# Retention and a rational FFN on one core: later chunks go through TensorE in pairs, with zero products in its waits and a new table of ranks

## The chip, the cores and the metric

The kernel runs on one core of one Trainium2 chip. The metric is the time of one execution on the device, in microseconds (us). Engines are named as in the profile: PE is TensorE (PEld its weight loads), DVE is VectorE, ACT is ScalarE, POOL is GpSimd, SP is SyncE, whose queue issues every DMA of this kernel.

## The reference

Retention (linear attention with a decay per head) over 4 batches, 8 heads, 768 tokens and 64 dimensions; its output, as 3072 tokens of 512 values, goes through a feed-forward layer of 2048 with a rational activation.

```python
gamma = 1.0 - 2.0 ** (-5.0 - np.arange(H))
for t in range(S):
    state = gamma[None, :, None, None] * state + np.einsum('bhd,bhe->bhde', k[:, :, t], v[:, :, t])
    y[:, :, t] = scale * np.einsum('bhd,bhde->bhe', q[:, :, t], state)
...
h = x @ w_in
P = a[0] + a[1] * h + a[2] * h**2 + a[3] * h**3
Q = 1.0 + np.abs(b[0]) * np.abs(h) + np.abs(b[1]) * h**2
out = (P / (Q + 1e-06)) @ w_out
```

## The kernel before

**Chunks.** The 768 tokens are cut into 6 chunks of 128, and chunk i = 4n + b is the n-th of batch b. The four first chunks (n = 0) have no state and go in a form of their own. Each of the 20 later chunks makes two bursts of small 64x64 products on PE, four of which run side by side in quarters of the array. The first burst (L350, L358) holds the scores of both halves of the chunk (16 products into pa) and the outer products of k and v (16, or 8 in the last chunk, into the other half of the same two banks). Then DVE masks the scores (aT), adds the outer products to the state (mid, after), all in steps of 256 columns. The second burst (L376, 32 products into px) recalls from state and mid and multiplies aT with v. DVE scales px, ACT rounds it into xh, DVE takes the remainder xl; POOL scales k ahead of it (L439) and the state behind it.

**Slots.** Four chunks give 512 columns of x. The FFN is a list of 96 slots k, each one column block n of x and one block f of 128 hidden units. In slot k the hidden block, called h_k here, is twelve products of 512 columns into a bank ph (L665: w high with xh, w high with xl, w low with xh). ACT, POOL and DVE turn ph into g: an Abs (L718), a linear step called the second activation here (L727 on ACT or L723 on POOL), a third (L733), a product on POOL (L738), five steps on DVE and two more on ACT (L747, L750); ACT rounds g into gh (L762), POOL takes the remainder gl (L766). The output block, O_k here, is again twelve products, into four banks po (L680: gh with w high, gh with w low, gl with w high). There are two banks ph, so h_(k+2) waits until slot k is done with its bank. The first 32 slots go through the column blocks 0 and 1 in halves of 8 hidden blocks.

**Weights.** w_in and w_out come as 64-bit numbers, 0.52 MB for each of 32 blocks. Each is decoded: two ACT steps (L625, L629), two DVE steps (L635, L638), a split into the high part on ACT (L644) and the rest on POOL (L647).

**The order.** Nothing runs in the order in which it is written. Each piece of work is a step with engines, a cost, its predecessors, buffers and a rank; `Plan.order` (below) picks at each time the ready step with the lowest rank on the engine that is free first, and emits it. The tables LOADS, RANKS and OFFSETS set the ranks. The engines then run their own instructions strictly in the emitted order. Before the first h the planner puts bf16 products of zeros into PE's waits (L893).

**Banks.** Of the eight PSUM banks, two are for ph, four for po, and two (b2, b3) for everything else: pa, px, pk. Until a given number of h blocks has begun (EARLY), the po banks serve too.

Of the kernel before, what the change touches and what calls it, by code (L numbers as in the profile page):

```python
# [7 lines left out]
F32 = mybir.dt.float32  # L8
# [16 lines left out]
COLD = 2600, 3200  # L25
# [19 lines left out]
class Plan:  # L45
# [10 lines left out]
    def step(  # L56
        self, engines, cost, run, after=(), rank=0.0, takes=(), uses=(), tiled=False, kind=None
    ):
        rank += OFFSETS.get(kind, 0.0)
# [70 lines left out]
    def order(self, emit):  # L130
# [6 lines left out]
        open_ = []  # L137

        def enter(x):
            x.known = 0  # L140
            for a, early in x.after:
                x.known = max(x.known, a.start if early is None else a.end - early + WAKE)
            open_.append(x)
# [5 lines left out]
        while left:  # L149
# [5 lines left out]
            by_engine = {}  # L155
            for x in open_:
                t = self.ready(x)
                if t is None:
                    continue
                for e in x.engines:  # L160
# [15 lines left out]
            open_.remove(x)  # L176
# [8 lines left out]
def tile_retention_rational_ffn(  # L185
# [29 lines left out]
    HF = NF // 2  # L215
# [20 lines left out]
    zeros = ff.tile([P, DM], F32, name="o", bufs=BUFS["o"]).bitcast(BF16)[:, :TB]  # L236
# [27 lines left out]
    def pairs():  # L264
        names = free_banks()
        return [names[i : i + 2] for i in range(0, len(names) - 1, 2)]

# [77 lines left out]
    def scores_outer(st, last):  # L345
        for aj in range(NP):
            for r in range(2):
                for e in range(2):
                    h = 4 * (aj // 2) + 2 * r + aj % 2
                    nc.tensor.matmul(  # L350
                        st["pa"][e][half(r), aj], st["kT"][half(e), h], st["qT"][half(e), h],
                        start=True, stop=True, skip_group_check=True,
                    )
        for aj in range(NP):
            for r in range(2):
                for e in range(1 if last else 2):
                    h = 4 * (aj // 2) + 2 * r + aj % 2
                    nc.tensor.matmul(  # L358
                        st["pk"][e][half(r), aj], st["k"][half(e), h], st["v"][half(e), h],
# [3 lines left out]
    def recall_values(st, own):  # L363
        for what in range(2):
            for e in range(2):
                for a in range(2):
                    for j in range(2):
                        for r in range(2):
                            aj, h = 2 * a + j, 4 * a + 2 * r + j
                            if what:  # L370
                                x = st["v"][half(r), h] if r == e else st["v2"][half(r), aj]
                                y = st["aT"][e][half(r), aj]
                            else:
                                x = (st["mid"] if e else own)[half(r), aj]
                                y = st["qT"][half(r), h] if r == e else st["q2T"][half(r), aj]
                            nc.tensor.matmul(  # L376
                                st["px"][r][half(j), a * P + e * D : a * P + (e + 1) * D], x, y,
                                start=(not what and e == 0 and a == 0), stop=what == 1,
                                skip_group_check=True,
                            )  # L380
# [3 lines left out]
    def x_parts(st, i, r):  # L384
        n, b = divmod(i, B)
        t = slice(b * P, (b + 1) * P)
        xh, xl = (y.rearrange("p (a r) t -> p r a t", r=2)[:, r, :, t] for y in x_tiles[n])
        return st["px"][r][:, : TB // 2].rearrange("p (a t) -> p a t", t=P), xh, xl
# [19 lines left out]
    def attention(i, rank, load_rank, gate):  # L408

        st, (n, b) = {}, divmod(i, B)  # L410
        c, own = n, state[:, b]
        buf, got = {}, {}

        def part(m, src, shape, rank):
            tag = BORROWED.get(i, {}).get(m)
            buf[m] = Buffer(tag or m)

            def dst():
                if tag:
                    full = ff.tile([P, TB], F32, name=m, tag=tag, bufs=BUFS[tag])  # L420
                    st[m] = full.rearrange("p (a b) -> p a b", b=shape[2])
                else:
                    st[m] = at.tile(shape, F32, name=m, bufs=BUFS[m])
                return st[m]

            nbytes = 4 * P * shape[1] * shape[2]
            got[m], _ = load(dst, lambda: src[b, c - 1] if c else src[b], nbytes, rank, [buf[m]])

        kshape = [P, H, D] if c else [P, NP, P]
        part("kT", kT if c else kT0, kshape, load_rank)  # L430
        part("qT", qT if c else qT0, kshape, load_rank + 0.01)
        part("v", v if c else v0, [P, H, D], load_rank + 0.02)
        part("k", kk if c else kk0, [P, H, D], load_rank + 0.015 if c else LATER)
        if c:
            part("q2T", q2T, [P, NP, D], load_rank + 0.03)
            part("v2", v2, [P, NP, D], load_rank + 0.04)

        def scale_k(_):
            nc.gpsimd.tensor_mul(  # L439
                st["k"], st["k"], kdec_sb[:, min(c, 1)].unsqueeze(2).broadcast_to([P, H, D])  # L440
            )

        K = step(
            ("POOL",), (1000, 1043), scale_k, [got["k"], ready["few"]], rank, uses=[buf["k"]], kind="V"
        )

        pa, aT = Buffer("psum", pairs), [Buffer("aT") for _ in range(2)]
        before = bursts.get(i - 2 if i < B else i - 1)
        turn = before and (before, None)

        def run_scores(_):
            banks = [psum(pa, s, "pa") for s in range(2)]
            if c:
                st["pa"], st["pk"] = (
                    [x[:, y].rearrange("p (h t) -> p h t", t=D) for x in banks]
                    for y in (slice(0, TB // 2), slice(TB // 2, TB))
                )
                scores_outer(st, c == C - 1)
            else:
                st["pa"] = [x[:, : 6 * D].rearrange("p (j t) -> p j t", t=3 * D) for x in banks]  # L460
                first_scores(st)

        S = step(
            ("PE",), (900, 800) if c else (830, 700), run_scores,
            [got["kT"], got["qT"], gate, turn] + ([K, got["v"]] if c else []), rank, [pa],
            [buf[m] for m in (("kT", "qT", "k", "v") if c else ("kT", "qT"))], True, "S",
        )
        M = []
        for s in range(2):

            def mask(_, s=s):
                aT_ = at.tile([P, 6 * D], F32, name="aT", bufs=BUFS["aT"])
                if c:
                    by = mask_sb[:, s]
                    aT_ = aT_[:, : 4 * D].rearrange("p (h t) -> p h t", t=D)
                else:
                    by = masks[s].rearrange("p (j t) -> p j t", t=3 * D)
                    aT_ = aT_.rearrange("p (j t) -> p j t", t=3 * D)
                st.setdefault("aT", {})[s] = aT_
                nc.vector.tensor_mul(aT_, st["pa"][s], by)  # L480
# [3 lines left out]
                    ("DVE",), (335, 420) if c else (470, 550), mask,  # L484
                    [S, ready["mask"] if c else mask_loads[s]], rank,
# [557 lines left out]
```

## Time and profile before

| | |
|---|---|
| median of 3 runs | 621.4 us (620.86 to 621.76) |
| the profiled execution | 622.29 us |
| its span, first to last instruction | 620.5 us |
| mean granted TensorE clock | 0.989 |
| PE busy | 601.5 us, 97% |
| DVE, ACT, POOL busy | 72%, 68%, 56% |
| HBM read, written | 50.21 MB, 8.39 MB |
| weights, per block | 512 KB, 7.6 us from issue to landing |

The span is what the views below divide; the 1.8 us between it and the time of the execution lie around it. A busy time counts overlapping instructions once. In a group's row the mean is that of one instruction from start to end; products on PE overlap, so twelve of them take less than twelve means. The chain of waits is followed back from the last instruction, and its rows add up without overlap.

### The profile page before, as it was taken

How to read it: one execution, taken by the hardware profiler on the slowest of the kernel's cores; microseconds unless marked ns; L12 is line 12 of the kernel's file. 1: busy time of each engine (PE TensorE's matmuls, PEld its weight loads, DVE VectorE, ACT ScalarE, POOL GpSimd, SP SyncE). 2: the span in 40 equal slices, each digit the busy share in tenths (PEclk: the TensorE clock that was granted, in tenths of full speed). 3: DMA queues.
4: the chain of work that ended last, by engine and by line, in shares of the span. 5: the costliest groups of instructions: out<-in, count | busy, mean ns of one | idle time of the engine just before them, and what ended most of it. 6: DMA issues, size and time to landing. Idle time of an engine off the chain costs nothing.

```text
span 620.5 us, 13030 instructions
## 1 busy us (share of the span) xinstructions
PE 601.5 (97%) x5155; PEld 485.9 (78%) x5155; DVE 449.1 (72%) x743; ACT 421.6 (68%) x700; POOL 347.0 (56%) x303
## 2 busy tenths in 40 slices
PE   8858999999999999999999999999999999999997
PEld 4736877888887888887888888888888888888885
DVE  3689788999979867767766776667766666666662
ACT  1687779999965555565666766666666666776772
POOL 2387677998867675654544545444444444444442
PEclk9968999999999999999999999999999999999999
DMA  8999631003024330224411222112311100100001
GB/s 304 411 414 414 233 86 69 1 1 135 1 86 155 120 120 17 69 69 121 130 43 52 103 73 66 35 52 69 120 52 36 34 1 0 61 9 1 1 0 69
DMA packets 30733, 59.44 MB, mean 96 GB/s; under 512 B 3536, under 2 KB 8912, under 8 KB 30672
## 3 DMA queue, kind: packets, MB, share of 16 engines
q1 hardware_dynamic: 30672, 58.62, 26.8%
q8 instruction: 40, 0.66, 0.4%
q14 instruction: 21, 0.17, 0.1%
HBM read 50.21 MB, written 8.39 MB: 94 GB/s over the span
## 4 chain that ended last, share of the span: by engine, by line
PE 88%; POOL 2%; DVE 1%; ACT 1%; issue 1%; POOLq 0%; DVEq 0%; ACTq 0%
PE po L680 41%; PE ph L665 41%; PE px L376 3%; PE pa L350 2%; PE pa L358 1%; POOL w L647 1%; POOL gl L766 1%; POOL q L738 0%; ACT ph L750 0%; POOL s L723 0%; ACT s L747 0%; DVE q L754 0%; DVE p L756 0%; DVE ph L755 0%; ACT gh L762 0%
## 5 line engine op out<-in xcount | busy, mean ns | idle before, releaser
L665 PE MATMUL ph<-xh,w 128*128 128x512 f32 (+2 forms) x776 | 209.0, 392 | 3.4 <-DVE p L756 2.3
L680 PE MATMUL po<-w,gh 128*128 128x512 f32 x768 | 203.4, 397 | 6.2 <-ACT gh L762 5.3
L738 POOL TENSOR_TENSOR q<-q,s 128x512 f32<-128x512 f32 x96 | 124.2, 1294 | 147.0 <-ACT s L727 144.3
L680 PEld LDWEIGHTS po<-w,gh 128*128 128x128 f32 x768 | 143.0, 189 | 37.6 <-ACT gh L762 5.4
L665 PEld LDWEIGHTS ph<-xh,w 128*128 128x128 f32 x776 | 144.2, 189 | 35.3 <-DVE p L756 4.1
L766 POOL TENSOR_TENSOR gl<-p,gh 128x512 fp32r<-128x512 f32 x96 | 124.1, 1292 | 27.5 <-ACT gh L762 18.0
L754 DVE SCALAR_TENSOR_TENSOR q<-q,small,ph 128x512 f32<-128x512 f32 x96 | 71.6, 745 | 93.7 <-ACT ph L750 91.8
L718 ACT ACTIVATE q<-ph 128x512 f32<-128x512 f32 x96 | 57.3, 596 | 87.7 <-PE ph L665 87.3
L680 PE MATMUL po<-w,gl 128*128 128x512 f32 x384 | 111.6, 392 | 0.9 <-POOL gl L766 0.9
L665 PE MATMUL ph<-xl,w 128*128 128x512 f32 (+2 forms) x388 | 104.0, 390 | 0.0
L747 ACT ACTIVATE s<-q,small 128x512 f32<-128x512 f32 x96 | 69.5, 724 | 49.2 <-POOL q L738 49.2
L741 DVE TENSOR_TENSOR p<-ph,p 128x512 f32<-128x512 f32 x96 | 65.8, 685 | 30.2 <-ACT p L733 29.1
L680 PEld LDWEIGHTS po<-w,gl 128*128 128x128 f32 x384 | 72.6, 189 | 16.8 <-POOL gl L766 1.7
L665 PEld LDWEIGHTS ph<-xl,w 128*128 128x128 f32 x388 | 73.2, 189 | 15.3
L733 ACT ACTIVATE p<-ph,small 128x512 f32<-128x512 f32 x96 | 74.3, 774 | 2.1 <-POOL gl L766 2.1
L742 DVE SCALAR_TENSOR_TENSOR p<-p,small,ph 128x512 f32<-128x512 f32 x96 | 71.8, 748 | 3.4
L762 ACT CAST gh<-p 128x512 fp32r<-128x512 f32 x96 | 59.2, 617 | 20.1 <-PE po L680 13.0
L755 DVE SCALAR_TENSOR_TENSOR ph<-p,small,ph 128x512 f32<-128x512 f32 x96 | 71.9, 749 | 0.0
L756 DVE SCALAR_TENSOR_TENSOR p<-q,ph 128x512 f32<-128x512 f32 x96 | 65.9, 686 | 3.3
L750 ACT ACTIVATE ph<-s 128x512 f32<-128x512 f32 x96 | 57.8, 602 | 3.7
L647 POOL TENSOR_TENSOR w<-t,w 128x512 fp32r<-128x512 f32 x32 | 41.2, 1293 | 19.8 <-ACT w L644 10.8
L727 ACT ACTIVATE s<-q,small 128x512 f32<-128x512 f32 x61 | 49.7, 814 | 0.3
(53 smaller groups left out, 445.8 us busy)
## 6 DMA issues: line engine op xcount, KB each, us to landing
raw<-in_w_in SPq DMA_DIRECT2D x16, 512.0 KB, 7.6
raw<-in_w_out SPq DMA_DIRECT2D x16, 512.0 KB, 7.8
kT<-in_kT SPq DMA_DIRECT2D x24, 256.0 KB, 3.3
qT<-in_qT SPq DMA_DIRECT2D x24, 256.0 KB, 3.2
v<-in_v SPq DMA_DIRECT2D x24, 256.0 KB, 3.9
k<-in_k SPq DMA_DIRECT2D x24, 256.0 KB, 3.6
out<-o SPq DMA_DIRECT2D x24, 256.0 KB, 2.6
q2T<-in_q2T SPq DMA_DIRECT2D x20, 128.0 KB, 3.2
```

The costliest lines, as they stand in the source:

```text
L665: nc.tensor.matmul(cell["ph"][:, t0:t1], w[0, f][:, part, kt * P : (kt + 1) * P], x[:, kt, t0:t1], start=(i == 0), stop=(i == 3 * NP - 1),)
L680: nc.tensor.matmul(o_tiles[n][tt], g_[:, tt * P : (tt + 1) * P], w[1, f][:, part], start=(first and m == 0), stop=(last and m == 2),)
L733: nc.scalar.activation(cell["p"], cell["ph"], AF.Identity, bias=par_sb[:, 2:3], scale=par_sb[:, 3:4])
L738: nc.gpsimd.tensor_mul(cell["q"], cell["q"], cell["s"])
L741: nc.vector.tensor_mul(cell["p"], cell["ph"], cell["p"])
L742: nc.vector.scalar_tensor_tensor(cell["p"], cell["p"], par_sb[:, 1:2], cell["ph"], ALU.add, ALU.mult)
L747: nc.scalar.activation(cell["s"], cell["q"], AF.Abs_reciprocal_sqrt, bias=qcon[:, 0:1])
L754: nc.vector.scalar_tensor_tensor(q_, q_, qcon[:, 0:1], ph_, ALU.add, ALU.mult)
L755: nc.vector.scalar_tensor_tensor(ph_, p_, par_sb[:, 0:1], ph_, ALU.add, ALU.mult)
L756: nc.vector.scalar_tensor_tensor(p_, q_, 2.0, ph_, ALU.subtract, ALU.mult, reverse0=True)
L762: nc.scalar.copy(cell["gh"], cell["p"])
L766: nc.gpsimd.tensor_sub(cell["gl"], cell["p"], cell["gh"].bitcast(F32))
```

## The change

Chunks 4 to 23 are taken in pairs (two batches of the same n). A pair makes three bursts: the scores of both chunks (32 products, a bank for each half), the outer products of both (32, or 16 at the end, in banks of their own), the recall of both (64). Each DVE, ACT and POOL step behind them covers both chunks, so 512 columns and not 256. There are only two banks for pa, pk and px of one pair behind the start, so each burst enters the banks that the one before has left. Some loads share buffers with tiles that are free by then (`more`, `again`).

```diff
-    def scores_outer(st, last):
+    def scores(st):
+        for x in range(st["n"]):
+            for aj, r, h in heads():
...
+    def outer(st, last):
+        for x in range(st["n"]):
...
+    def later_chunks(i, n, rank, load_rank, gate):
+        more = "o" if c == 1 else "t"
+        small_ops = ((335, 420), (571, 613)) if n == 1 else ((600, 685), (1000, 1043))
...
+        pa = Buffer("psum", pairs)
+        pk = Buffer("psum", pairs) if n == 2 else pa
...
+        if n == 2:
+            O = step(
+                ("PE",), (1000, 900), run_outer, [*K, *ins["v"], (S, None)], rank, [pk],
+                held["k"] + held["v"], True, "S",
+            )
...
+                by = mask_sb[:, e].unsqueeze(1).broadcast_to([P, n, NP, D])
+                nc.vector.tensor_mul(st["aT"][e], st["pa"][e], by)
...
+        R = step(
+            ("PE",), (1000, 900) if n == 1 else (1860, 1760), run_rest,
...
+                many = 2 if built >= PAIRS else 1
+                later_chunks(
+                    built, many, RANKS.get(built, starts[built] + 0.5), LOADS.get(built, starts[built] / 100),
+                    gate,
+                )
```

Products of zeros now go into every wait of PE that the planner expects to be over 0.9 us, also behind the first h: into the bank that comes next, or with start off into an open po bank, to which they add zero.

```diff
-                for _ in range(min(10, int(gap / 430))):
-                    nc.tensor.matmul(idle, zeros[:, :P], zeros, start=True, stop=True)
+            if engine == "PE" and gap > 900:
+                spare[0] = min(12, int(gap / FILL))
+                if not begun(1):
...
+                    fill(idle, True)
+                elif open_po:
+                    fill(open_po[0], False)
```

In the emitted order there are 38 of them: 12 and 10 among the first four chunks, 11 ahead of h_1, 3 ahead of O_0 and 2 ahead of the scores of the second pair. Before there were 23, all ahead of h_0.

The tables are new: LOADS, RANKS, OFFSETS, a nudge for each of some 400 steps, three buffers t in place of two, EARLY 4, and a list of the slots whose second activation is on POOL.

```diff
-        engines = ("ACT", "POOL") if k < SHARED else ("ACT",)
-        A2 = turn("A2", step(engines, {"ACT": (720, 820), "POOL": (771, 771)}, a2, [A1, ready["babs"]], k, [s], [q], kind="A2"))
+        A2 = turn("A2", step(by("A2", k), {"ACT": (720, 820), "POOL": (771, 771)}, a2, [A1, ready["babs"]], k, [s], [q], kind="A2"))
...
+        rank += OFFSETS.get(kind, 0.0) + NUDGES.get(len(self.steps), 0.0)
...
+ENGINES = {
+    ("A2", 0): "POOL", ("A2", 7): "POOL", ("A2", 8): "POOL", ("A2", 9): "POOL",
```

That list has 10 slots (0, 7, 8, 9, 15, 16, 21, 23, 26, 29); before, POOL had 35 second activations, all in the first 40 slots, among them every one of the slots 10 to 21. The first weight of w_in is now the fourth load on SP (it was the twentieth). The last copies out of po begin on DVE and end on ACT (before the other way round). An alternative form of DVE's steps (`aside`) is in the code, but no slot of the list uses it.

What the tables do is seen in the order of instructions. First PE where the chunks with n = 3 begin (pa are scores, pk outer products, px recall). Before, behind h_38, chunk 12:

```order
L350 MATMUL pa<-qT,kT 64x64 x16
L358 MATMUL pa<-v,k 64x64 x16
L680 MATMUL po<-w,gh 128x512 x8
L680 MATMUL po<-w,gl 128x512 x4
L665 MATMUL ph<-xh,w 128x512 x4
L665 MATMUL ph<-xl,w 128x512 x4
L665 MATMUL ph<-xh,w 128x512 x4
L680 MATMUL po<-w,gh 128x512 x8
L680 MATMUL po<-w,gl 128x512 x4
L665 MATMUL ph<-xh,w 128x512 x4
L665 MATMUL ph<-xl,w 128x512 x4
L665 MATMUL ph<-xh,w 128x512 x4
```

Here the recall burst of the one chunk follows. Now, behind h_39, chunks 12 and 13 together:

```order
L369 MATMUL pa<-qT,kT 64x64 x32
L821 MATMUL po<-w,gh 128x512 x8
L821 MATMUL po<-w,gl 128x512 x4
L378 MATMUL pk<-v,k 64x64 x32
L804 MATMUL ph<-xh,w 128x512 x4
L804 MATMUL ph<-xl,w 128x512 x4
L804 MATMUL ph<-xh,w 128x512 x4
L399 MATMUL px<-qT,state 64x64
L399 MATMUL px<-q2T,state 64x64
```

The outer products have a burst of their own, one block behind the scores, and the recall of both chunks stands one block behind that.

Second, ACT from the first Abs to the first gh (q, p, s, gh are slot steps, t, u, w decode steps). Before, without its first two rows:

```order
L733 ACTIVATE p<-ph,small 128x512
L625 ACTIVATE t<-raw,small 128x512
L629 ACTIVATE u<-raw 128x512
L718 ACTIVATE q<-ph 128x512
L644 CAST w<-t 128x512
L747 ACTIVATE s<-q,small 128x512
L750 ACTIVATE ph<-s 128x512
L733 ACTIVATE p<-ph,small 128x512
L569 CAST xh<-px 128x2x128 x2
L644 CAST w<-t 128x512
L625 ACTIVATE t<-raw,small 128x512
L762 CAST gh<-p 128x512
```

Now, without its first row:

```order
L763 ACTIVATE t<-raw,small 128x512
L879 ACTIVATE p<-ph,small 128x512
L782 CAST w<-t 128x512
L763 ACTIVATE t<-raw,small 128x512
L767 ACTIVATE u<-raw 128x512
L899 ACTIVATE s<-q,small 128x512
L900 ACTIVATE ph<-s 128x512
L767 ACTIVATE u<-raw 128x512
L782 CAST w<-t 128x512
L763 ACTIVATE t<-raw,small 128x512
L767 ACTIVATE u<-raw 128x512
L919 CAST gh<-p 128x512
```

The second slot's steps and the rounding of x have left the way to the first gh; decode steps stand there, and the first w behind the Abs is the one that h_1 needs.

Third, the end of PE, from the last hidden block on. Before:

```order
L665 MATMUL ph<-xh,w 128x512 x4
L680 MATMUL po<-w,gh 128x512 x8
L680 MATMUL po<-w,gl 128x512 x4
L680 MATMUL po<-w,gh 128x512 x8
L680 MATMUL po<-w,gl 128x512 x4
L680 MATMUL po<-w,gh 128x512 x8
L680 MATMUL po<-w,gl 128x512 x4
L680 MATMUL po<-w,gh 128x512 x8
L680 MATMUL po<-w,gl 128x512 x4
L680 MATMUL po<-w,gh 128x512 x2
L680 MATMUL po<-w,gl 128x512
```

Now:

```order
L804 MATMUL ph<-xh,w 128x512 x4
L821 MATMUL po<-w,gh 128x512 x8
L821 MATMUL po<-w,gl 128x512 x4
L821 MATMUL po<-w,gh 128x512 x8
L821 MATMUL po<-w,gl 128x512 x4
L821 MATMUL po<-w,gh 128x512 x8
L821 MATMUL po<-w,gl 128x512 x4
L821 MATMUL po<-w,gh 128x512 x2
L821 MATMUL po<-w,gl 128x512
```

Four output blocks follow the last hidden block in place of five; the last of them takes its products bank by bank, two with gh and one with gl each.

More of the change, by code (lines that the diff above doesn't have):

```diff
@@ L154, in order @@
                         self.claims.append((x, frozenset(b.options()[0])))
-            by_engine = {}
-            for x in open_:
+            by_engine, some = {}, 0
+            for x in open_ + loads:
+                if some == 6:
+                    break
                 t = self.ready(x)
@@ L266, in pairs, with fill @@
         return [names[i : i + 2] for i in range(0, len(names) - 1, 2)]
+    open_po, spare = [], [0]
+    def fill(bank, start):
+        for _ in range(spare[0]):
+            nc.tensor.matmul(
+                bank, zeros, zeros.unsqueeze(1).broadcast_to([P, TB // P, P]), start=start, stop=start,
+                skip_group_check=True,
+            )
+        spare[0] = 0
     def load(dst, src, nbytes, rank, takes=(), uses=(), after=()):
@@ L363, in recall_values @@
     def recall_values(st, own):
[L364 to L380, printed above, removed]
@@ L443, in attention @@
[L443 to L449, printed above, removed]
+                st[m] = block(tag, m).rearrange("p (a b) -> p a b", b=shape[2])
+                return st[m]
+            got[m], _ = load(dst, lambda: src[i], 4 * P * shape[1] * shape[2], rank, [buf[m]])
@@ L451, in run_scores @@
+        part("kT", kT0, [P, NP, P], load_rank)
+        part("qT", qT0, [P, NP, P], load_rank + 0.01)
+        part("v", v0, [P, H, D], load_rank + 0.02)
+        part("k", kk0, [P, H, D], LATER)
+        K = scale_k(st, 0, buf["k"], got["k"], rank, lambda: st["k"])
+        pa, aT = Buffer("psum", pairs), [Buffer("o") for _ in range(2)]
+        before = bursts.get(i - 2)
         def run_scores(_):
             banks = [psum(pa, s, "pa") for s in range(2)]
[L453 to L461, printed above, removed]
+            fill(banks[0], True)
+            st["pa"] = [x[:, : 6 * D].rearrange("p (j t) -> p j t", t=3 * D) for x in banks]
+            first_scores(st)
@@ L580, in attention @@
-        x_done[i] = done
+                by = sdec_sb.unsqueeze(1).unsqueeze(3).broadcast_to([P, n, NP, D])
+                nc.gpsimd.tensor_mul(own, st["after"], by)
+            new = step(("POOL",), small_ops[1], scale_state, [U, R], rank, uses=[after_], kind="U")
+            for x in range(n):
+                last_state[b + x] = new
+        x_steps(st, i, n, R, px, rank, True)
     def first_states(b, rank, gate):
@@ L683, in gemm_out, with turn_of @@
             )
-    stores, sums, halves = {}, {}, {}
+    stores, sums, parts = {}, {}, {}
+    def turn_of(n, f):
+        return next(((a, b) for m, a, b in TURNS if m == n and a <= f < b), (0, NF))
     def turn(name, x):
```

447 lines of the change are left out of this document (284 added, 163 removed), and 96 rows, old and new, of tables (LOADS, NUDGES, OFFSETS, RANKS).

## The prediction

> **What bounds the kernel now.** I read the page first (busy times, slices, chain), then the busy times by stretch, then the waits. From the page:
>
> ```profile
> PE 601.5 (97%) x5155; PEld 485.9 (78%) x5155; DVE 449.1 (72%) x743; ACT 421.6 (68%) x700; POOL 347.0 (56%) x303
> ...
> PE   8858999999999999999999999999999999999997
> ...
> PEclk9968999999999999999999999999999999999999
> DMA  8999631003024330224411222112311100100001
> ...
> PE 88%; POOL 2%; DVE 1%; ACT 1%; issue 1%; POOLq 0%; DVEq 0%; ACTq 0%
> ```
>
> TensorE (PE) is the bound: 88% of the chain, and full in every slice but the first four and the last. Only two things can shorten the kernel: less work on PE, or fewer holes and a better clock at the start. The stretches show how much lies there (columns: us, busy PE, PEld, DVE, ACT, POOL with counts, granted clock, DMA share, GB/s):
>
> ```profile
> 0.00:23.00 23.00, 18.31 (x343) 11.71 (x343) 9.92 (x25) 6.80 (x16) 4.25 (x8) 1.00 0.94 338
> 23.00:37.20 14.20, 8.92 (x164) 7.69 (x164) 11.52 (x21) 11.97 (x22) 12.10 (x12) 0.89 1.03 413
> 37.20:62.40 25.20, 21.57 (x188) 16.15 (x189) 21.93 (x38) 19.76 (x33) 17.94 (x16) 0.79 1.04 415
> 62.40:95.40 33.00, 31.79 (x370) 24.68 (x368) 26.31 (x47) 25.76 (x45) 23.26 (x22) 1.00 0.43 146
> 100.20:616.40 516.20, 516.14 (x4073) 421.64 (x4071) 374.67 (x608) 352.96 (x580) 286.12 (x245) 1.00 0.18 57
> ```
>
> After 100.2 PE has 0.06 us of holes in 516. Between 23.0 (first big product) and 95.4 it is idle for 72.4 - (8.92 + 21.57 + 31.79) = **10.1 us**, and the clock is low in the second and third row. The chain of waits gives the price of one block and one burst (start, us, what):
>
> ```profile
> 100.22 2.72 PE ph L665 x12
> ...
> 178.31 2.72 PE ph L665 x12
> 181.02 1.09 PE px L376 x64
> 182.12 2.95 PE ph L665 x12
> ```
>
> A block of twelve 512-column products is 2.72 us. A burst of 64 records (32 products of 64x64, two records each) is 1.09, and the block behind it takes 2.95, so a burst costs 1.09 + 0.23 = **1.32 us**. Up to 95.4 PE did h0 to h9, 6.33 output blocks and 8 bursts: 16.33 x 2.72 + 8 x 1.32 = 55.0 us of work in 72.4. So 17.4 us were lost, 10.1 idle and some 7.3 by the clock. One stretch and one block show the clock:
>
> ```profile
> 38.00:40.00 2.00, 1.06 (x4) 0.50 1.07 414
> ...
> 57.97 4.61 PE ph L665 x12
> ```
>
> The first follows the long hole before the first output block, the second a hole of 2 us. What ended the holes (engine, line, what it waited for: total, times, longest), and what ScalarE (ACT) waited for in the same 20 to 110 us:
>
> ```profile
> PE po L680 <- ACT gh L762: 5.3, 1, 5.3
> PE ph L665 <- DVE p L756: 2.3, 2, 2.0
> ...
> ACT q L718 <- PE ph L665: 5.1, 5, 2.0
> ACT t L625 <- POOL w L647: 3.6, 5, 0.9
> ```
>
> **Bursts.** Two chunks took four bursts (scores with outer products, recall, twice); now they take three: scores 64 records, outer 64, recall 128. Inside a burst (records of one recall burst, and the block behind it):
>
> ```profile
> 69.30 0.27 PE L376 MATMUL px<-qT,state 64*64 64x64 f32 x1
> 69.40 0.22 PE L376 MATMUL px<-qT,state 64*64 64x64 f32 x1
> 69.46 0.22 PE L376 MATMUL px<-qT,state 64*64 64x64 f32 x1
> 69.81 0.65 PE L376 MATMUL px<-aT,v 64*64 64x64 f32 x32
> 70.39 2.11 PE L680 MATMUL po<-w,gh 128*128 128x512 f32 x8
> ```
>
> Groups of four records follow each other by 0.058 us (69.40, 69.46, and on to 69.81), so 16 groups are 0.93; the other 1.32 - 0.93 = 0.39 is entering and leaving. One entry and exit per pair goes: 10 pairs x 0.39 = **-3.9 us**, of which two pairs (-0.8) lie in the ramp and eight (**-3.1**) behind it. Bounds: 0 if a merged burst stalls inside, -5 if all of 0.5 goes.
>
> **The ramp.** In the order, PE has up to the end of O7 ten hidden blocks, eight output blocks and the bursts of two pairs: 18 x 2.72 + 2 x (1.32 + 1.32 + 2.25) = 58.7 us. Before, O7 ended at 100.22. The start of h0 stays:
>
> ```profile
> 23.02 0.98 PE L665 MATMUL ph<-xh,w 128*128 128x384 f32 x4 [1.10 <-ACT w L644]
> ```
>
> Its weight is now loaded fourth and decoded while ACT idles, which would win the 1.1 us; but the last chunk of the first four now comes 0.52 MB later at 338 GB/s, 1.5 us. I take 23.0. Then the waits. h1 needs its weight: on ACT a first activation, a decode step, the third activation and the split stand between h0 and it, and on POOL its rest stands behind a scaling of k:
>
> ```profile
> 28.34 0.59 ACT L718 ACTIVATE q<-ph 128x512 f32<-128x512 f32 x1
> 90.25 0.62 ACT L762 CAST gh<-p 128x512 fp32r<-128x512 f32 x1 [1.17 <-DVE p L756]
> L439 POOL TENSOR_TENSOR k<-k,small 128x512 f32<-128x512 f32 x24 | 25.0, 1045 | 19.7 <-DMA k<-in_k 16.5 <-PE po L680 2.0 <-DVE aT L480 1.1
> ```
>
> In the stretch from 37.2 ACT does one instruction per 19.76 / 33 = 0.60 us, so four are 2.4; the scaling may add its 1.05. With the two, h1 loses 3.5 us, where before the hole in front of O0 was 5.3 (O0 now has h2 and a whole recall burst ahead of it, so its cover is 5 us more). For later waits on a freed bank I take the old 2.3 (2.0 and 0.3, in front of h3 or h4). The old one of 2.0 was followed by the block of 4.61 instead of 2.95, 1.7 of clock; I take 0 for that and keep 1.7 as a bound, since which of the two new holes is as long isn't known. Waits 5.8: O7 ends at 23.0 + 58.7 + 5.8 = 87.5, against 100.22 (the block at 100.22 is h10, right behind O7): **-12.7**. That needs ACT: up to slot 7's gh it has 94 instructions from the first activation on (85 before), 94 x 0.60 = 56.4, from h0's end at 23.0 + 2.8 = 25.8 to 82.2; O7 starts at 84.8. So ACT has 2.6 us to spare. Before, it used 90.87 - 28.34 = 62.5 us for 85 x 0.60 = 51.0: it waited 11.5. Fewer holes on PE mean fewer such waits (5.1 of them were for PE), so I put 4.3 in their place, 1.7 over what is spare: **-11.0** for the ramp. Bounds: all waits gone, 81.7 instead of 87.5, gives -18.5; ACT waiting 11.5 as before gives -12.7 + 8.9 = -3.8.
>
> [...]
>
> **Zero products.** Sixteen stand behind h0: eleven before h1, three before O0, two before the scores of the second pair. Their rows of before:
>
> ```profile
> 1.19 4.02 PE L893 MATMUL idle<-o 128*128 128x512 bf16 x9 [1.19 <-DVE small L243]
> ...
> 8.72 0.82 PE L893 MATMUL idle<-o 128*128 128x512 bf16 x3
> ```
>
> 0.27 to 0.45 us each. The eleven (3.0 to 5.0 us) lie in the 3.5 us that h1 waits anyway; if that cover is missing they are work: 0 to 5 us, I take 0. What they buy is in the sum already: no block at half clock. That zeros hold the clock is shown by the first row of the stretches, 1.00 to 23.0 with them.
>
> **Steps over 512 columns.** Cheaper, off PE:
>
> ```profile
> L741 DVE TENSOR_TENSOR p<-ph,p 128x512 f32<-128x512 f32 x96 | 65.8, 685 | 30.2 <-ACT p L733 29.1
> L573 DVE TENSOR_TENSOR xl<-px,xh 128x256 fp32r<-128x256 f32 x48 | 18.1, 415 | 0.5 <-ACT xh L569 0.5
> ```
>
> 685 ns for one against 2 x 415, eight per pair: 1.2 us of DVE saved per pair, worth nothing while PE is full. But between two bursts of a pair two such steps must empty the only two free banks: 1.4 us, with one to two blocks of 2.95 in between. I take +0.5 in all (0 to 14, below).
>
> **The tail.** The order has four output blocks behind the last hidden block, before five:
>
> ```profile
> 602.75 13.61 PE po L680 x60
> ...
> 602.79 0.60 ACT L718 ACTIVATE q<-ph 128x512 f32<-128x512 f32 x1 [0.71 <-PE ph L665]
> ...
> 609.85 0.62 ACT L762 CAST gh<-p 128x512 fp32r<-128x512 f32 x1 [2.33 <-DVE p L756]
> 610.89 1.29 POOL L766 TENSOR_TENSOR gl<-p,gh 128x512 fp32r<-128x512 f32 x1 [3.52 <-ACT gh L762]
> ```
>
> The last gl is there at 612.18, 9.4 us behind h95. Three blocks cover 8.16, and two products of the last block 0.45: PE waits **+1.0** (0 to 1.5), where the fifth block hid it.
>
> **Sum.** -11.0 - 3.1 + 0.5 + 1.0 = -12.6. The profiled execution was 622.29 (span 620.5 and 1.8 around it): 609.7; the median of the runs, 621.4, is 0.9 lower: **608.8 us**.
>
> **Rivals.**
> - *ACT takes the ramp back* (615.5). From slot 8 to 20 the second activation is on ACT nine times where it was on POOL, and on POOL twice where it was on ACT; ACT already ran at
>
> ```profile
> 100.00:160.00 60.00, 57.43 (x97) 1.00 0.14 51
> ```
>
>   96%. By the count slot 20's gh stands 211 instructions behind the first activation, 126.6 us, so at 152.4; O20 starts at 87.5 + 2.7 + 12 x 5.44 = 155.5: 3.1 to spare, less the waits. With the old waits of 11.5, O20 is 8.4 late: the ramp is worth 4.3, and the time 621.4 - 4.3 - 3.1 + 1.5 = 615.5. Against: fewer decodes are left after slot 9 than before. Chance 0.13.
> - *Only the bursts pay* (621.4 - 3.9 + 1.5 = 619): loads come late, since the order of the weights is new and DMA is full until 62 (1.03, 1.04).
>
> ```profile
> k<-in_k SPq DMA_DIRECT2D x24, 256.0 KB, 3.6
> ```
>
>   The k of chunk 7 has 21.9 MB ahead of it: 23 + (21.9 - 7.8) / 0.415 = 57, and 3.6 us to land, where its burst stands at about 62. Thin. Chance 0.06, and 0.05 that late handovers (next) eat these 2.4 us too and nothing measurable is left.
> - *Slower: DVE hands the banks over too late.* Masks must leave the banks before the outer products enter, and the sums before recall. If DVE has just begun a slot's five steps (the row of the first has 685 ns; 3.4 in all), two steps end 3.4 + 1.4 = 4.8 us behind the burst, with 2.95 of cover: 1.9 late. Twenty handovers at 1.0 on average are +20: 608.8 + 20 = 629. It decides from 0.65 us each (13 us in twenty). Against it: a burst on PE also gives DVE 1.3 to 2.3 us more, and before, four steps of 0.41 were done under one block with 0.06 us of holes. [...] Chance 0.08.
> - *The zeros stand in the way* (613): the waits that they fill aren't there, and sixteen at 0.27 are +4.3. Inside the range; 0.10 of the forecast's chance.
>
> **How the numbers follow.** Forecast (604 to 614) 0.63; better than 604, 0.05; ACT 0.13; only the bursts 0.06; no difference 0.05; slower 0.08. Faster by over 0.2% (1.2 us, about what a measurement of this kernel can tell from no change) 0.63 + 0.05 + 0.13 + 0.06 = 0.87, within it 0.05, slower 0.08. The range 604 to 619.5 leaves out 0.05 below and 0.13 above.
>
> **What would show it.** O7 ends near 88 us, and the row of the granted clock is 9 in all slices (ramp); recall bursts of about 2.0 us with 2.95 behind, three per pair (bursts); a wait of the last output block for gl of about 1 us (tail); PE holes behind 100 us under 1 us (handovers). Wrong: clock at 0.5 in the ramp, PE waiting for ACT between 90 and 160, or for DVE in front of outer products or recall.

## The result, and the profile after

| | before | after |
|---|---|---|
| median, runs of one chip | 621.52 us (620.86 to 621.76, 4 runs) | 614.12 us (611.93 to 615.83, 4 runs) |
| the profiled execution, its span | 622.29, 620.5 us | 615.09, 613.3 us |
| h10 begins (O7 ends) | 100.06 | 94.45, forecast 87.5 to 89.2 |
| from there to the end of the span | 520.4 | 518.8, forecast 518.8 |

The ratio is 0.988 (95% interval 0.9845 to 0.9917): faster by 7.4 us, where 12.6 had been forecast. The last two rows of the table say where the difference lies: behind h10 the forecast holds to 0.1 us, and the ramp, which is the stretch ahead of it, gave about half of its 11.0. (Of the two forecasts of h10, 87.5 has the waits on PE alone, 89.2 also the 1.7 us that the sum adds for ACT.) The page of the changed kernel:

```profile
PE 597.7 (97%) x5170; PEld 485.3 (79%) x5170; DVE 442.2 (72%) x665; ACT 433.6 (71%) x705; POOL 326.0 (53%) x270
...
PE   7789999999999999999999999999999999999997
...
PEclk9899999999999999999999999999999999999999
...
PE 82%; DMA 9%; ACT 3%; issue 2%; POOL 1%; SPq 1%; DVE 1%; POOLq 0%; DVEq 0%
```

PE has its deep holes in three slices now and not in four, but the clock still falls in the second one (8, which the forecast wanted to be 9). Next the busy times by stretch (us, busy PE, PEld, DVE, ACT, POOL, granted clock, DMA share, GB/s), of after, and in the last row of before:

```profile
22.39:29.82 7.43, 5.15 (x29) 5.00 (x25) 5.01 (x9) 4.40 (x9) 2.57 (x2) 0.77 1.04 408
29.82:48.00 18.18, 15.02 (x300) 10.77 (x300) 15.32 (x24) 17.64 (x30) 14.65 (x13) 1.00 1.03 407
48.00:62.00 14.00, 13.94 (x121) 11.03 (x120) 13.64 (x22) 13.94 (x24) 9.29 (x8) 1.00 1.04 407
62.00:94.40 32.40, 32.09 (x316) 25.76 (x316) 30.13 (x47) 29.26 (x51) 26.11 (x23) 1.00 0.46 173
94.40:609.70 515.30, 514.06 (x4073) 421.39 (x4072) 369.15 (x544) 361.41 (x582) 267.85 (x217) 1.00 0.17 57
```

```profile
100.06:616.40 516.34, 516.28 (x4073) 421.77 (x4071) 374.67 (x608) 353.10 (x580) 286.26 (x245) 1.00 0.18 57
```

h0 alone takes 7.43 us, at a clock of 0.77. At full clock and without a hole it takes 3.6 (e5 and e8 below): it is 24 products, twelve of 384 columns and twelve of 128, and not twelve of 512. From h0's end to 48 PE is idle for 3.2 us while ACT is busy for 17.64 of 18.18. After that PE is full. PE's timeline at h0 (start, us, what, and in brackets the idle time before it and the releaser that the profile infers):

```profile
22.39 0.96 PE L804 MATMUL ph<-xh,w 128*128 128x384 f32 x4
25.64 1.44 PE L804 MATMUL ph<-xl,w 128*128 128x384 f32 x4 [2.28 <-DVE u L773]
```

The second row names a decode step of DVE. The name is a coincidence: the products of the first 384 columns need the xl of the first three chunks, and DVE had ended the last of these at 22.67; the decode step that is named ran from 24.74 to 25.43. PE's weight loads tell more:

```profile
23.03 0.19 PEld L804 LDWEIGHTS ph<-xl,w 128*128 128x128 f32 x1
25.64 0.93 PEld L804 LDWEIGHTS ph<-xl,w 128*128 128x128 f32 x3 [2.43 <-issue]
```

The second weight load uses a weight with which products had begun at 22.39, and waits for nothing that the profile shows ("issue"). The reading that follows is that PE had no instructions. The DMA queues by stretch (packets, MB, share of 16 engines), first from 17 to 23.2, then from 23.2 to 24.3:

```profile
q1 hardware_dynamic: 933, 2.57, 103.7%
```

```profile
q1 hardware_dynamic: 126, 0.44, 99.2%
q8 instruction: 1, 0.02, 5.5%
```

q8 carries instructions: 40 packets of 16,384 bytes in the whole execution, 0.66 MB. PE has 10,417 (5170 products, as many weight loads, and 77 of its sequencer, semaphore waits above all), which is about 63 bytes for each and some 260 to a packet. Here are the first packets beside what PE had begun (a place is one of these instructions, counted from PE's first):

```
packet   transfer        PE stood still at place, until      after the packet's end
1        15.99 - 16.92   449   18.29   (0.65 us)             1.37
2        23.26 - 24.23   705   25.64   (2.28 us)             1.42
3        29.05 - 30.02   -
4        42.12 - 43.07   1217  44.53   (0.56 us)             1.46
10       122.64 - 123.66 -
```

449, 705 and 1217 are 193 + 256 n, which fits packets of 256 instructions, and PE stood still where packet n had yet to come. In the quiet part packet n begins when PE is about at place 256 n - 86 (2474 at the tenth, 10152 at the fortieth). By that the second packet would be due at place 426, which PE passed at 16.9; it began at 23.26, while the loads kept DMA at 1.05. Behind the hole the clock was at 0.50:

```profile
26.00:27.00 1.00, 1.00 (x5) 1.00 (x4) 0.86 (x3) 0.79 (x2) 0.39 (x2) 0.50 1.07 420
27.00:28.00 1.00, 1.00 (x5) 1.00 (x4) 0.68 (x1) 0.00 (x0) 1.00 (x1) 0.50 1.01 408
```

PE stood still for the three packets of the table and for none of the other 37 of this trace. No packet begins more than 298 places ahead of the first place that it feeds, and PE ran dry 279 places behind the point where the second packet fell due (705 - 426).

The bursts and the tail look as forecast (the chain of waits; L1271 on POOL's queue is the last gl, for which the last output block waits):

```profile
191.40 1.09 PE pk L378 x64
192.49 2.95 PE ph L804 x12
195.44 2.02 PE px L399 x128
197.46 2.95 PE po L821 x12
...
602.49 3.20 issue
605.69 1.32 POOLq L1271
607.01 0.04 issue
607.05 2.60 PE po L821 x10
```

### The profile page after: what moved, and what is told of

It reads as the page before. It is cut to its first block, busy times and chain, and to the rows that moved or that the text cites. A ratio compares the mean times of both kernels' runs of the same rounds, so it can differ in the third digit from the quotient of the medians.

```text
span 613.3 us, 12814 instructions
## 1 busy us (share of the span) xinstructions
PE 597.7 (97%) x5170; PEld 485.3 (79%) x5170; DVE 442.2 (72%) x665; ACT 433.6 (71%) x705; POOL 326.0 (53%) x270
## 4 chain that ended last, share of the span: by engine, by line
PE 82%; DMA 9%; ACT 3%; issue 2%; POOL 1%; SPq 1%; DVE 1%; POOLq 0%; DVEq 0%
PE ph L804 39%; PE po L821 38%; DMA k<-in_k 4%; PE px L399 3%; DMA raw<-in_w_in 2%; PE pk L378 2%; DMA kT<-in_kT 2%; PE pa L369 1%; SPq L292 1%; DMA v<-in_v 1%; POOL q L884 1%; ACT s L899 1%; ACT s L873 0%; ACT ph L900 0%; ACT t L763 0%
## 5 line engine op out<-in xcount | busy, mean ns | idle before, releaser
L821 PE MATMUL po<-w,gh 128*128 128x512 f32 x768 | 200.2, 392 | 0.3 <-POOL w L785 0.3
L899 ACT ACTIVATE s<-q,small 128x512 f32<-128x512 f32 x96 | 69.5, 724 | 66.4 <-POOL q L884 66.4
L873 ACT ACTIVATE s<-q,small 128x512 f32<-128x512 f32 x86 | 69.9, 812 | 0.0
```

The lines of the kernel that those rows point to most:

```text
L821: nc.tensor.matmul(o_tiles[n][tt], g_[:, tt * P : (tt + 1) * P], w[1, f][:, part], start=(first and m == 0), stop=(last and m == 2),)
L873: nc.scalar.activation(cell["s"], cell["q"], AF.Identity, bias=babs[:, 0:1], scale=babs[:, 1:2])
L899: nc.scalar.activation(s_, cell["q"], AF.Abs_reciprocal_sqrt, bias=qcon[:, 0:1])
```

## The experiments

The theories: **F**, instruction packets come late while DMA is full, and PE stands still at places 193 + 256 n; **D**, DVE's decode steps stand ahead of what h0 needs; **L**, loads bind the ramp; **A**, the decode steps on ACT and DVE bind it; **C**, the zero products matter, for the clock or as dead weight. All twelve runs, each with the ratio to runs of the kernel before on the same chip. Fetch holes are those at places 193 + 256 n, up to h10. "h0 ends" is the end of its last product; products overlap, so what follows may begin 0.16 us before it. All columns but the last two are of the one profiled execution, which in e1, e9, e12 and e4 was 1.4 to 2.5 us slower than the median and in e5 2.0 faster:

| run | fetch holes, us | h0 ends | h1 begins | h10 begins | h1 to h10 | h10 to end | median | ratio (interval) |
|---|---|---|---|---|---|---|---|---|
| after | 0.65, 2.28, 0.56 | 30.0 | 32.48 | 94.45 | 62.0 | 518.8 | 614.12 | 0.988 (0.985-0.992) |
| e10, the same again | 1.31, 1.10, 0.78, 0.57 | 27.6 | 30.14 | 93.00 | 62.9 | 518.9 | 614.61 | 0.990 (0.988-0.991) |
| e1 | 1.62, 0.57 | 29.2 | 31.75 | 93.74 | 62.0 | 519.6 | 613.66 | 0.989 (0.987-0.991) |
| e2 | 1.30, 1.10, 0.64 | 28.3 | 30.85 | 93.23 | 62.4 | 519.5 | 613.92 | 0.989 (0.987-0.992) |
| e6 | 0.93, 1.10, 0.58 | 27.4 | 29.94 | 92.25 | 62.3 | 522.2 | 615.21 | 0.991 (0.989-0.994) |
| e8 | 0.34, 0.23 | 25.7 | 29.70 | 92.28 | 62.6 | 519.0 | 613.37 | 0.988 (0.986-0.990) |
| e9 | 0.75 | 26.0 | 30.04 | 93.08 | 63.0 | 520.9 | 614.37 | 0.989 (0.987-0.991) |
| e11 | 0.42, 1.18, 0.58, 0.71 | 26.7 | 28.74 | 89.28 | 60.5 | 519.9 | 611.03 | 0.985 (0.982-0.987) |
| e12 | 0.94, 0.56 | 25.8 | 28.33 | 90.31 | 62.0 | 521.7 | 611.78 | 0.986 (0.983-0.988) |
| e5 | none | 24.7 | 27.71 | 94.79 | 67.1 | 524.1 | 622.68 | 1.002 (1.000-1.004) |
| e4 | 2.83 | 27.9 | 29.74 | 109.97 | 80.2 | 525.3 | 634.65 | 1.023 (1.021-1.025) |
| e7 | 1.09 | 28.2 | 28.09 | 111.33 | 83.2 | 527.1 | 639.91 | 1.030 (1.028-1.032) |
| e3 (kernel before, edited) | 2.53 | 30.5 | 30.32 | 102.21 | 71.9 | 520.3 | 624.05 | 1.005 (1.003-1.007) |

**e1: ten zero products fewer ahead of h0.**

```diff
                 if not begun(1):
+                    spare[0] -= 5
```

> The changed kernel with ten of the 22 zero products ahead of h0 taken out (five of each group), so that every later instruction of TensorE stands 20 places earlier in its stream; nothing else is moved. Theory F (instruction fetch): the stream comes in packets of 16,384 bytes, and PE stood still for 2.28 us inside h0 because the packet asked for while DMA was full landed only at 24.23. With the stream 20 places earlier, the same place of the work is reached with instructions in hand: no hole inside h0, h0 at 2.95 instead of 7.43 us and no half clock behind it; the first of the three fetch holes (0.65 us, at 17.6 to 18.3) grows to about 1.5, the third (0.8 at 44) stays. Time 610.5 (609.5 to 612). Rival D (DVE's decode steps stand ahead of the xl products): the hole of 2.28 us stays, 614 us. Rival C (zeros are needed for the clock): half clock ahead of h0 now, 615 to 617.

The hole in h0 is gone, the first is 1.62 at the same place 449, the third stayed at 1217. (In e10, the same program as after, the first hole is 1.31, so only part of its growth from 0.65 is the edit's.) D falls. A row of PE and one of DVE:

```profile
25.60 1.48 PE L804 MATMUL ph<-xl,w 128*128 128x384 f32 x4
```

```profile
26.16 0.70 DVE L773 SCALAR_TENSOR_TENSOR u<-u,t 128x512 uint32<-128x512 uint32 x1
```

The xl products began before the decode step (the second u) that the profile of after had named as their releaser. The vanished hole alone proves less for F, since h0 began only at 24.15, and in after the second packet had landed at 24.23; the stronger evidence is that the other two holes kept their places in the stream. The time did not follow: the clock fell behind the first hole instead (0.50 from 22 to 26), h0's first products took 1.65 us in place of 0.96, and h1 began only 0.7 us earlier. Ten products less moved the hole and did not remove it.

**e3: the kernel before with a longer stream.**

```diff
                     idle = ps.tile([P, TB], F32, name="idle", tag="b1")
+                    for _ in range(16):
+                        nc.tensor.matmul(idle[:, :D], zeros[:, :P], zeros[:, :D], start=True, stop=True)
```

> The kernel before with 16 more small zero products (64 columns) as PE's first work, where it waits for loads anyway; every later instruction stands 32 places later in its stream. Theory F: the kernel before had no fetch hole only because of where its packets ended (its second packet landed 0.5 us ahead of need); now PE stands still for about 1.8 us at 20 to 22 us, in the bursts of the first chunks, and h0 starts 0.7 to 1.8 later: 622.2 to 623.3 against 621.5. Rivals D and A (loads late): no hole, no difference.

PE's timeline of it:

```profile
22.24 0.45 PE L326 MATMUL px<-aT,v 128*64 128x64 f32 x7 [2.53 <-issue]
...
24.47 1.65 PE L665 MATMUL ph<-xh,w 128*128 128x384 f32 x4 [0.30 <-ACT w L644]
```

The hole that the kernel before did not have, in the burst that F named, and half clock behind it (0.50 from 24 to 26; 1.65 us in place of 0.98). It stands at place 702 of the records, and three products ahead of it have no record, so at 705. Sixteen small products where PE waits anyway made the kernel 3.2 us slower (0.5%, interval 0.3 to 0.7), more than the 0.7 to 1.8 expected, since F's price left out the clock.

**e5: both first outer bursts behind h0.**

```diff
+            if k == 0:
+                for x in held:
+                    x.after.append((gemms_in[0], None))
```

> The changed kernel with the outer products of the four first chunks (two bursts of 64 records, 128 places each with their weight loads taken together) moved from ahead of h0 to between h0 and h1, where eleven zero products stood; later steps follow the planner. Theory F: 122 fewer places ahead of h0, so neither of the two fetch holes ahead of h1 stays (the first packet now ends in the last first chunk's recall, the second inside the moved bursts, in the time that h1 waits anyway): h0 starts at 20.5 to 22 and takes 2.95; h1 still starts at 32 to 33, when its weight is ready, so little comes out of it: 612 to 615. If h1 were bound by h0 and not by its weight, it would start at 28 and the time be 610. The hole in the recall burst near 43 stays. Rival D (decode steps on DVE hold h0): a hole of over 1 us stays inside h0.

No fetch hole is left, h0 begins at 21.07 and h1 at 27.71, 4.8 us earlier than in after and 2.4 earlier than in e10: F again. But the planner then put the rest in another order, in which PE waits for DVE (4.2 us ahead of products into ph, 3.4 ahead of zero products), and all of it was lost: 622.68. h1 was bound by h0's end through ACT, against the expectation that its weight would hold it at 32.

**e8 and e9: one outer burst moved, every other order kept.** e8 moves the outer products of chunks 2 and 3 behind h0 and puts six zero products where eleven stood; e9 has 24 short ones there.

```diff
+            if x in moved and gemms_in[0].start is None:
+                kept_back.append((x, engine))
+                return
...
+            if x is gemms_in[1]:
+                spare[0] = 6
             x.run(engine)
```

> The changed kernel with every engine's order kept, but for one burst: the outer products of chunks 2 and 3 (32 records, 64 places with their weight loads) and the sum behind them go from ahead of h0 to right behind it, and six zero products instead of eleven stand between them and h1. Theory F: ahead of h1 no fetch hole over 0.4 us; h0 starts near 21.2 and takes 2.95 at full clock, so ends near 24.2 (29.8 in the changed kernel). ACT then has slot 0's first activation at 26.9, when its decode steps are done, and h1's weight 2.4 later: h1 at 29.3 to 30 (32.5). The hole in the recall burst of the first pair stays, since the stream there is only 10 places shorter. If what stands behind follows, h10 starts 2.5 to 3 earlier than 94.4 and the time is 611 to 611.6; if loads bind the ramp behind h1 (theory L), h10 gains under 1 and the time is 613.5. Rival D: the hole in h0 stays.

> The same, but 24 zero products of 128 columns in place of the six of 512 (about as long, 26 places longer in the stream than the changed kernel from h1 on). Theory F: the packet boundary that fell into the first recall burst now falls ahead of it, so that this hole (0.6 to 0.8 us) goes too; h10 0.5 earlier than in the run before it. Otherwise the same.

> The changed kernel once more, beside the two above on the same chip, as the measure for differences of 1 to 3 us: 0.988 of the kernel before, with fetch holes of about 0.65, 2.3 and 0.6 us.

As F says, both holes ahead of h1 are gone in e8 and e9, and in e9 the one at 1217 too; another at 1985, which only some runs show, came to 0.75. In place of the first hole PE now waits for a load, in e8 1.1 us and in e9 1.6 (in e8 the profile names a step of DVE, but the load's last piece came at 18.69 and the product began at 18.83). The row of e9:

```profile
19.19 1.03 PE L329 MATMUL pa<-qT,kT 64*64 64x128 f32 x30 [1.61 <-DMA kT<-in_kT]
```

So that hole had stood where the load of the last first chunk was late anyway, and h0 begins only 0.7 us (e8) and 0.4 (e9) earlier than in e10, though 1.1 us of products had been moved off ahead of it. Beside e10, h0 ends 1.9 us earlier in e8, h1 begins 0.4 earlier, and h10 0.7 earlier; in e9 h1 begins 0.1 earlier and h10 0.1 later. Beside after, whose clock had fallen, h10 is 2.2 and 1.4 earlier. These are single executions: the holes cost between nothing and 0.7 us where the clock holds and some 1.4 to 2.2 where it falls, and the 611 that was expected did not come. Theory L or A has the rest: from h1 to h10 it is 62 to 63 us in all seven runs with this order and the full decoding, whether the hole in the recall burst is there or not. The medians, 613.37 and 614.37 against 614.61, show no difference that five or six runs can tell apart.

**e2: no zero products behind h0.**

```diff
-                spare[0] = min(12, int(gap / FILL))
+                spare[0] = 0 if begun(1) else min(12, int(gap / FILL))
```

> The changed kernel without the sixteen zero products behind h0 (11 ahead of h1, 3 ahead of O0, 2 ahead of the second pair's scores). As predicted they lie in waits and cost nothing: h1 starts at 32.5 as before, the half clock lasts through h1 or not, 613.5 to 616. Rival (zeros stand in the way): h1 starts up to 2.5 us earlier, 611 to 612. Theory F adds: the stream behind h0 is 22 to 32 places shorter, so the fetch hole in the recall burst at 44 us moves, within 0.3 us of the same length.

```profile
30.85 2.07 PE L804 MATMUL ph<-xh,w 128*128 128x512 f32 x4 [2.50 <-ACT w L782]
...
32.00:33.00 1.00, 1.00 (x4) 0.81 (x3) 0.87 (x2) 0.97 (x3) 1.00 (x2) 0.50 1.10 414
```

(The second row is of the stretches.) h1 begins when its weight is ready, as it did with the eleven zeros; without them it runs at half clock (0.50, where after has 1.00), yet h10 stays within 0.3 us of e10, because what follows h1 waits for something else. The zeros do hold the clock, then, and nothing of it reaches h10: theory C is no cause of the miss.

**e6: second activations of slots 10 to 20 on POOL.**

```diff
+    ("A2", 10): "POOL", ("A2", 11): "POOL", ("A2", 12): "POOL", ...
```

> The changed kernel with the second activation of slots 10 to 20 on POOL, as in the kernel before, and not on ACT. The prediction's rival that ACT takes the ramp back says 2 to 6 us faster (ACT has nine instructions of 0.8 us fewer between 100 and 160). The trace of the changed kernel has no hole of PE there: by it nothing is won, 613 to 615; POOL's later 0.77 us steps may cost up to 2.

The stretch from 100 to 160, of after and then of e6:

```profile
100.00:160.00 60.00, 60.00 (x266) 49.29 (x265) 53.51 (x80) 59.24 (x100) 44.14 (x36) 1.00 0.05 18
```

```profile
100.00:160.00 60.00, 59.21 (x257) 47.76 (x256) 54.68 (x82) 53.84 (x92) 53.33 (x48) 1.00 0.15 49
```

ACT at 99% had cost PE nothing, which refutes the prediction's rival at the place that it named. With ACT relieved to 90% and POOL at 89%, PE had its first holes there, 0.8 us.

**e11 and e12: what holds h1 to h10.** e11 leaves out one ACT and one DVE step of each decoding (the first lines below), e12 half of each weight's load (the second).

```diff
-            nc.scalar.activation(cell["t"], byte, AF.Identity, bias=lcon[:, 0:1], scale=1.0 / 32)
...
-            nc.vector.scalar_tensor_tensor(
-                u_, u_, 3, t_, ALU.logical_shift_left, ALU.bitwise_or
-            )
```

```diff
-        got, _ = load(dst, lambda: (w_in, w_out)[m][f], 8 * P * DM, load_rank)
+        got, _ = load(part, lambda: (w_in, w_out)[m][f][:, :DM], 8 * P * DM, load_rank)
```

> The changed kernel with one ACT step (0.77 us) and one of the two DVE steps (0.70 us) of every weight's decoding left out (the low three bits of a weight's mantissa and the shift that makes room for them); the order of everything else is kept. It asks what holds the stretch from h1 to h10, which took 62.0 to 63.0 us in every order with the changed tables so far, with fetch holes in it or without, against 58.2 in the prediction. Theory A (decode steps on ACT and DVE bind it): it falls to 56 to 59, and the time to 608 to 611. Theory L (loads bind it): 61.5 to 63, and 613 to 614.5. Theory F: the holes ahead of h1 and in the recall burst stay, since loads are the same.

> The changed kernel with half of each weight loaded (0.26 MB in place of 0.52 MB), and the decode steps reading this half twice, so that half of each weight's values are missing; all steps and their order are kept. Theory F: DMA is full for a shorter time, instruction packets land sooner, and the holes ahead of h1 shrink from about 4 us to under 2, the one in the recall burst goes; h0 ends 1 to 3 us earlier. Theory L (loads bind h1 to h10): this stretch falls from 62 to under 59, time 608 to 611. Theory A: it stays at 61 to 63, time 611.5 to 613.5.

The stretch from 30 to 48 of e10, e11 and e12:

```profile
30.00:48.00 18.00, 14.81 (x298) 11.68 (x298) 17.24 (x28) 17.64 (x31) 15.08 (x13) 1.00 1.04 411
```

```profile
30.00:48.00 18.00, 16.46 (x308) 12.87 (x307) 15.36 (x25) 16.08 (x28) 15.13 (x13) 1.00 1.04 411
```

```profile
30.00:48.00 18.00, 14.56 (x299) 11.53 (x299) 17.46 (x28) 17.66 (x31) 15.13 (x13) 1.00 0.71 241
```

With the loads halved DMA is at 0.71, PE has no more work done than before, and h1 to h10 stays at 62.0: L is refuted for this stretch. With the decoding shorter ACT falls from 98% to 89% and PE rises from 14.81 to 16.46; h1 to h10 falls by 2.3 us to 60.5, and with the earlier h1 the ramp is 3.7 us shorter. That is A's direction and less than its 56 to 59. PE itself is busy for 58.3 us between h1 and h10 in e11 and for 58.8 in e10, so what the decode steps held is the holes: 4.0 us in e10, 2.3 in e11. e12 is also F's test from the other side: the fetch holes ahead of h1 are 1.5 us together (2.9 and 2.4 in after and e10), and those at 1217 and 1985 are gone. With less to load h0 begins at 21.45 and not at 22.70, and h1 1.8 us earlier.

**e4 and e7: pairs and tables apart.** e4 takes the chunks in pairs with the tables of the kernel before (and its rule for the zero products, without nudges), e7 single chunks with the new tables. The lines below are of e7; e4 changes the tables themselves.

```diff
-PAIRS = 4
...
+PAIRS = 24
```

> Pairs of chunks with the tables of the kernel before (loads, ranks, offsets, second activations shared with POOL, zero products ahead of h0 alone, no nudges; three buffers t, which the pairs need). Theory of the prediction: the bursts give 0.39 us per pair, 3.9 in all, whatever the tables, 617 to 619. Rival (pairs need their own tables: handovers of two banks cost): 620 to 625, with PE waiting for DVE ahead of outer products or recall.

> The changed kernel with single chunks again, ranks and loads of a pair for both of its chunks, every nudge on the step that had it (those of the chunks' own steps left out). Behind h10 the eight pairs cost eight more entries and exits: +3.1 us from h10's start to the end (518.9 in the changed kernel, so 522.0) if a burst's price is as predicted, 519 if the bursts give nothing. The ramp's waits are left open (its order was made for pairs): 617 to 630 in all.

Neither is a sum of parts: 634.65, beyond what either theory had for e4, and 639.91, with 527.0 behind h10 where 519 to 522.0 had been expected. In e4 PE waits for DVE's last step of a slot, ahead of products into ph, 11 times, 9.8 us; in both, h1 to h10 is over 80 us. As a price of the bursts they are inconclusive. What they show is that the pairs do not pay with the old tables, nor the new tables without the pairs.

## Why the prediction was right in sign and half wrong in size

The forecast was 608.8 us, and the measured 614.12 lies just outside the band of 604 to 614 that it gave the most likely outcome. It lies inside the whole range because that was drawn wide enough for the rivals (615.5 and 619). That the time is near the 615.5 of the rival on ACT is chance: e6 refutes what that rival said. **The step that was mis-sized is the ramp's -11.0**: it came to -5.6 (100.06 to 94.45), -7.1 in e10. By its own pieces:

- *h0 starts at 23.0*: 22.4. *h0 takes 2.8*: 7.4. This is the largest miss, +4.0 on h0's end. Of the 4.6 us that h0 took too long, 2.28 are a fetch hole and about 1.5 the half clock behind it. The other 0.8 is h0's own form of 24 products, 3.6 us, which the prediction counted as one block of 2.8. It had no term for any of the three. Its clock bound of 1.7 was about the right size, but it looked for the hole behind h0.
- *h1 waits 3.5*: 2.7. Right, and of the kind it named (first activation, decode, third activation, split on ACT).
- *From h1 on, 55.9 of work and 2.3 of waits, 58.2*: 62.0. The holes there were 0.54 (weight's low part, POOL), 1.11 and 0.83 (a bank that a decode step still held, DVE), 0.56 (fetch) and 0.31 (POOL), 3.35 instead of 2.3. The rest is on PE itself: five zero products, 1.0, and blocks that run longer behind holes and bursts, some 1.5.
- *ACT has 2.6 us to spare over the whole ramp*: a mean over a stage with two limits. ACT's 94 instructions were counted rightly: from the first activation to slot 7's gh they took 59.6 us (30.0 to 89.6), 3.2 over 56.4, where 4.3 had been put in. But from 30 to 62 ACT is busy for over 97% of the time, and from 48 on PE is full. e11 shows that the decode steps on ACT and DVE cause part of PE's holes between 30 and 48. Which of the two engines binds stays open, since e11 relieved both.

So h10 came 6.9 us late (94.45, 87.5 forecast): +4.0 at h0's end, -0.8 in h1's wait, +3.8 from h1 on. Without the fetch holes ahead of h1, and with the clock kept, only 2.2 of it is won back at h10 in e8 (1.4 in e9), because h1 then waits 4 us for its weight. The rest is with ACT's and DVE's steps and with the longer work on PE.

**Bursts -3.1, handovers +0.5, tail +1.0**: -1.6 forecast, -1.6 measured (520.4 to 518.8), with errors that cancel, so the agreement is luck. The shape is as predicted, recall bursts of 2.02 with 2.95 behind. PE's busy time from h10 on fell by 516.28 - 514.06 = 2.2, so 0.28 for each of the eight entries and exits saved, not 0.39. Holes came to 1.2 (515.30 - 514.06), of which 0.57 is the wait for the last gl (1.0 forecast), and what follows PE's last product is 0.5 shorter, which the prediction didn't look at. The last copy, on ACT now, is 0.1 of it (0.58 us, 0.69 on DVE before); the rest lies behind that copy.

**The rival of late handovers** was right about where, wrong about what and how much. In the ramp one burst waits for DVE, the outer products of the first pair, for a bank that a decode step still holds:

```profile
38.66 1.15 PE L378 MATMUL pk<-v,k 64*64 64x64 f32 x62 [1.11 <-DVE t L776]
```

Behind h10 no burst does. But PE waits there ahead of an h block close behind a pair's bursts, at 249 to 254, 288 to 292 and 388 to 390, in each execution at some of them, 0.2 to 1.8 us each. POOL of e9, ahead of a hole of 0.98 at 389.93:

```profile
383.96 1.04 POOL L548 TENSOR_TENSOR k<-k,small 128x512 f32<-128x512 f32 x1 [2.51 <-DMA k<-in_k]
384.96 1.29 POOL L886 TENSOR_TENSOR q<-q,s 128x512 f32<-128x512 f32 x1
```

In e10, where the same k was scaled at 381.74, the hole isn't there. POOL's scaling of the next pair's k waits for its load; the slot's product is queued behind it, ACT's and DVE's steps behind that, and the bank of ph comes free late. These holes are 0.5 us together in after and 3.4 in e12, where h10 begins 4.1 us earlier (521.7 behind h10, 518.8 in after). With the ramp 5.2 shorter in e11 they are 1.7, and in e8 1.1, so an earlier h10 does not always bring them. That k's load is the cause is read from the traces; no run moved it.

**Zero products at no cost**: right for those behind h0 (e2); those ahead of h0 also shift the stream's boundaries (e1, e3), which the prediction didn't consider. **ACT takes the ramp back between 100 and 160**: not so (e6), though ACT was full in an earlier stretch. Of the signs that the prediction named, the recall bursts of 2.02 came and the wait for gl at about half its size; O7's end near 88 and a clock of 9 in all slices did not, and two signs of being wrong did, the clock at 0.5 in the ramp and the wait for DVE in front of outer products.

## What to carry to other kernels

Where an engine with many small instructions stands still and the named releaser doesn't fit, look at whether its other queue says "issue", count its instructions up to each hole, and see whether the holes are a multiple of one number apart: here 256. Ahead of h1 such holes went here when fewer instructions stood ahead of h0 (e5, e8), and shrank when there was less to load (e12, 1.5 us in place of 2.4 in e10); the first was worth under 1 us at h10 while the clock held (e8, 0.7). Judge an engine's spare time stretch by stretch; a sum over a ramp hides the 32 us in which it is full. A gain ahead of a steady part may not all be kept: look whether the steady part's own loads are in time for it (argued here, not tested).

## What the runs showed of the hardware

- **PE's instructions come by DMA, and came late while DMA was full.** With DMA at 1.03 or more, packets 1 to 6 of after landed 4.3 to 8.0 us after PE had passed the place 256 n - 86; from the seventh on, with DMA at 0.5 or less on average, it was at most 2.4, but for one of 3.7. In after and its edited forms every hole of PE over 0.3 us, up to h10, that the profile puts down to "issue" stood at place 193 + 256 n, but for one of 0.53 in e5 (place 248). The three of after ended 1.37 to 1.46 us after a packet's end. A recall burst of 128 records has 256 places with its weight loads, and takes 2.0 us.
- **Half clock behind holes of about 2 us.** It followed holes of 2.00 (before), 2.28 (after), 2.53 (e3), 2.50 (e2) and one of 1.62 with another of 0.56 close behind (e1); it did not follow 1.31 and 1.10 (e10), 1.54 (e8) or 1.77 (e9). In before and after each stretch of half clock between the first full clock and PE's last product lasts 3.41 us or three times that: 25.51 to 28.92 in after, 34.14 to 44.38 and 58.04 to 61.45 in before. In the 3.41 us ahead of these three PE was, by its records, idle for 2.15, 2.20 and 2.00 us. In all other pieces of 3.41 us at full clock, laid end to end from where the clock rose, it was idle for 1.61 at most in these two traces. What decides between 1.6 and 2.0 they do not show.
- **One profile is one draw.** The same program had a hole of 2.28 us and half clock in one profiled execution and 1.10 us without it in another (h10 at 94.45 and 93.00), and its runs spread from 611.9 to 615.8. Of its nine executions four had a mean clock of 1.000 (611.9 to 614.6 us) and four one of 0.996 or 0.997 (613.2 to 615.8). An edit that seemed worth 0.7 us in the ramp of one trace was not to be seen in the medians.
